# An fp32 transformer block on one core: the second MLP product in seven sub-products for eight, three more operands streamed from DRAM, and a new pool layout

## The chip, the core and the metric

The kernel runs on one core of a Trainium2 chip. The metric is the device time of one execution in microseconds (us), lower is better. Engines are named as in the profile: PE is TensorE (PEld its weight loads, which overlap its matmuls), DVE is VectorE, ACT is ScalarE, POOL is GpSimd, and SP issues the DMAs.

## The reference

Input is `x` of 1 x 2048 tokens x 576 features, fp32. `mod = silu(c) @ w_mod` gives six rows of 576. Then

```python
h = layernorm(x) * (1 + ca) + sa
x = x + ga * linear_attention(h, wqkv, wo)     # 32 heads of 18, q/k through a positive map
h = layernorm(x) * (1 + cb) + sb
x = x + gb * (silu(h @ w1) @ w2)               # w1: 576 x 4608, w2: 4608 x 576
```

The last line is the MLP, and the change is all in it: the "up product" is h @ w1, the "down product" silu(..) @ w2.

## The kernel before

Every product is made of three passes. An fp32 operand is split into a rounded part "hi" (an fp32r copy on ACT) and a remainder "lo" (a subtraction, `sub_hi`, L62, on DVE), and a product is hi.hi + hi.lo + lo.hi, accumulated in PSUM. So an operand costs one ACT copy and one DVE subtraction, and a 128 x 128 x n product costs three matmuls.

**Stages.** LayerNorm, q/k/v and attention take the first 370 us or so. In them the MLP's first 256 hidden features (group 0) are already worked off as filler. From about 403 us on only the MLP is left, for hidden groups g = 1 to 17 of 256 features each (`NG` is 18). The tokens are two pairs p = 0, 1 of 1024, and a pair is two blocks i = 0, 1 of 512. One (g, p) is a `Unit`; there are 34 of them. At the head of the file the result rows lie in SBUF as `acc` (16 tiles of 128 tokens x 576), and every unit's down product is added to them.

**Up product (L912).** It is already done by seven products instead of eight (a Strassen scheme in Winograd's form): the 2 x 2 parts are feature halves of h and token blocks on one side, feature halves and hidden halves of w1 on the other. `ORDER = (1, 6, 2, 5, 7, 3, 4)` is the order of the products. A product is 6 matmuls of 128 x 512, and four of the seven carry 2 more for the odd 64 features: 50 matmuls a unit. The token operands of pair 0 lie in DRAM (`hd`) and are fetched by SP into three rooms of 1 to 1.25 MB (`Unit.fetch`, L901), each when the room's last reader on PE is done; those of pair 1 stay in SBUF (`hr`). The w1 operands of a group are made by `sums` (four POOL subtractions of 128 x 256, L859 to L862) and `up` (an ACT copy and a DVE subtraction for each of seven). `act` (L954 to L957) adds the PSUM result to an earlier partial result on DVE, applies silu on ACT, and splits the 128 x 512 result `f` into `hs` for the down product (ACT copy, DVE subtraction).

**Down product (L966).** It is the plain one. For each of the unit's 8 token tiles: 2 halves of the 576 output columns x 2 hidden halves x 3 passes = 12 matmuls of 128 x 288, into a `down` PSUM tile of two banks (two such tiles), and then one DVE addition of 128 x 576 into `acc` (L969). w2 is scaled by `gb` on DVE (L878) and split by ACT and DVE in two pieces of 128 x 576 a group (L881).

**Order.** The down products of a unit run between the up products of the next one. The code asks for one up, one down, and so on, but the framework's planner lays out the queues by its own estimate of times: in the trace it is mostly two ups, then two downs. Each engine then works strictly in its queue's order. Only w1 of the next group is loaded and split while pair 1 runs; both w1 and w2 land in the one `raw` buffer of pool `wm`.

The kernel's functions:

Of the kernel before, what the change touches and what calls it, by code (L numbers as in the profile page):

```python
# [15 lines left out]
P = 128  # L16
# [5 lines left out]
def kernel(ctx: ExitStack, tc, A_x, A_wqkv, A_wo, B_x, B_w1, B_w2, c, w_mod, out):  # L22
# [658 lines left out]
    def store_h(n, view, at=0):  # L681
        nc.sync.dma_start(hd[n][:, at : at + view.shape[1], :], f32(view))
# [4 lines left out]

    def store_s(pair, S, p):
        if pair == 0:
            store_h(p, S)  # L690
        else:
            hr[p] = S
# [12 lines left out]
    def turn_all(tb):  # L705
# [16 lines left out]
        else:  # L722
# [3 lines left out]
            S = [wqp.tile([P, 4, 512], F32R, name="S", bufs=2) for _ in range(2)]  # L726
# [21 lines left out]
        if tb % 2 == 1:  # L748
            e, o = h2[tb - 1], h2[tb]
            if pair == 0:  # L750
                store_h(1, e[:, 0:4, :])
                store_h(2, e[:, 4:9, :])
                store_h(4, o[:, ODD : ODD + 5, :])
                store_h(5, o[:, 9:10, :], 4)
                store_h(3, e[:, DIFF : DIFF + 1, :], 4)
            for n, p in ((0, 5), (1, 6)):
                store_s(pair, S[n], p)
            pool = wqp if pair == 0 else h2p
            S = [pool.tile([P, 4, 512], F32R, name="S", bufs=2) for _ in range(2)]
            for n, p in ((0, 7), (1, 3)):  # L760
                for c in range(2):
                    split_s(S[n], c, h32s[:, 2 * n + c])
                store_s(pair, S[n], p)
                yield
# [60 lines left out]
    wts = [wm.tile([P, 2, FW], F32R, name=f"wt{i}") for i in range(2)]  # L825
    for wt in wts:
        G.memset(f32(wt[64:128, 1, :]), 0.0)

    hr[1], hr[2], hr[4] = h2[2][:, 0:4, :], h2[2][:, 4:9, :], h2[3][:, ODD : ODD + 5, :]
    hr_tail = {2: htail(2), 5: htail(3), 3: h2[2][:, DIFF, :], 4: htail(3)}  # L830
    rst = rs.tile([P, 3, 2, P], F32, name="t")
    rooms = [rs.tile([P, 5, 512], F32R, name=f"room{i}") for i in range(2)][::-1] + [h2[3][:, 0:5, :]]
    rooms_used = 0
# [9 lines left out]
    class Weights:  # L843


        def __init__(self, g):
            self.f0, self.wt, self.w1, self.w2 = g * FW, wts[g % 2], {}, []

        def load1(self):
            r1 = self.r1 = wm.tile([P, KC + 1, FW], F32, name="raw")  # L850
# [5 lines left out]
        def sums(self):  # L856
            b11, b12, b21, b22 = (self.r1[:, 2 * j : 2 * j + 2, k * P : (k + 1) * P] for j in range(2) for k in range(2))
            t = rst
            G.tensor_sub(t[:, 0], b22, b12)  # L859
            G.tensor_sub(b12, b12, b11)  # L860
            G.tensor_sub(t[:, 1], b22, b12)
            G.tensor_sub(t[:, 2], b21, t[:, 1])  # L862
            self.b = {1: b11, 2: b21, 3: b22, 4: t[:, 2], 5: b12, 6: t[:, 1], 7: t[:, 0]}
            tail_w(self.wt, self.r1[:, KC, :])

        def up(self, n):
            w = self.w1[n] = wm.tile([P, 4, P], F32R, name="w1", bufs=8)
            A.copy(w[:, 0:2], self.b[n])  # L868
            sub_hi(w[:, 2:4], self.b[n], w[:, 0:2])

        def load2(self):
            r2 = wm.tile([P, KC + 1, FW], F32, name="raw").rearrange("p k f -> p (k f)")[:, : G2 * D]
# [3 lines left out]
        def down(self):  # L876
            r2 = self.r2
            V.tensor_mul(r2, r2, bc["gb"].unsqueeze(1).to_broadcast([P, G2, D]))  # L878
            for j in range(G2):
                w = pg.tile([P, 2, D], F32R, name="w2", bufs=3)  # L880
                A.copy(w[:, 0], r2[:, j])  # L881
                sub_hi(w[:, 1], r2[:, j], w[:, 0])
                self.w2.append(w)

    class Unit:


        def __init__(self, pair, w, last):
            self.pair, self.w, self.last = pair, w, last
            self.h = {}  # L890

        def fetch(self, n):

            nonlocal rooms_used
            if self.pair == 1:
                self.h[n] = hr[n], hr_tail.get(n)
            else:
                room = rooms[rooms_used % len(rooms)]
                rooms_used += 1
                m = hd[n].shape[1]  # L900
                nc.sync.dma_start(f32(room[:, :m, :]), hd[n])  # L901
                self.h[n] = room, room[:, 4, :]

        def passes(self, n, ps, first, k=None):

            h, tail = self.h[n]
# [4 lines left out]
            for i, (left, right) in enumerate(seq):  # L911
                T.matmul(ps, left, right, start=first and i == 0, stop=i == len(seq) - 1, skip_group_check=True)  # L912

        def up(self, n):
            def temp(name):
# [134 lines left out]
```

## Time and profile before

| | |
|---|---|
| median of 3 runs | 1238.67 us (1236.83 to 1239.61) |
| the profiled execution | 1238.09 us, span 1236.4 us, granted clock 0.992 |
| instructions | 18508 |
| PE / DVE / ACT / POOL busy | 97% / 63% / 34% / 10% of the span |
| HBM read / written | 188.17 MB / 13.11 MB |

The span is the time from the first to the last record of the core; the execution takes 1.7 us more. Busy shares count time in which at least one instruction of the engine runs. "idle before" of a group of instructions is time in which its engine had nothing else to do, with the engine and line that ended it. A line number can be that of a helper: all splits' subtractions are L62. Instructions of one engine overlap a little in the records, so the cost of one more instruction is read from back-to-back rows.

### The profile page before, as it was taken

The numbers are of one execution on the slowest core, as the hardware profiler recorded it, in microseconds if no ns is written. First come the engines' busy times: TensorE is split into PE (matmuls) and PEld (weight loads), VectorE is DVE, ScalarE is ACT, GpSimd is POOL, SyncE is SP. The second block draws the span as 40 slices with busy tenths as digits, with TensorE's granted clock in tenths as the row PEclk, the third lists the DMA queues.
The fourth block names the chain that finished last, engine by engine and source line by source line (L and its number), as shares of the span: only waits on it lengthen the run. The fifth ranks groups of instructions, "written<-read, shape, count | busy, mean of one in ns | idle before, by whom it ended". The sixth has DMA issues, their size and how long they took to land.

```text
span 1236.4 us, 18508 instructions
## 1 busy us (share of the span) xinstructions
PE 1195.0 (97%) x7569; PEld 1105.7 (89%) x7569; DVE 773.9 (63%) x1284; ACT 417.4 (34%) x780; POOL 125.8 (10%) x132
## 2 busy tenths in 40 slices
PE   5999999999898899999999999999999999999998
PEld 4999999899896699999999999999999999999998
DVE  6756754888858456466575565665665755656655
ACT  5434342235545323233233232332332332323321
POOL 3200000421501001001011000000010100100000
PEclk9999999999988999999999999999999999999999
DMA  9212300213423855563653744745636537446423
GB/s 265 99 52 74 111 1 1 80 39 115 173 84 118 324 190 185 211 245 118 263 194 141 291 160 175 252 155 202 254 117 251 205 138 284 160 175 257 158 79 153
DMA packets 48115, 202.48 MB, mean 164 GB/s; under 512 B 4570, under 2 KB 16094, under 8 KB 31902
## 3 DMA queue, kind: packets, MB, share of 16 engines
q1 hardware_dynamic: 48030, 201.30, 45.1%
q8 instruction: 59, 0.97, 0.3%
q14 instruction: 26, 0.21, 0.1%
HBM read 188.17 MB, written 13.11 MB: 163 GB/s over the span
## 4 chain that ended last, share of the span: by engine, by line
PE 85%; DVE 5%; issue 5%; DMA 3%; ACT 2%; POOL 1%; SPq 0%; POOLq 0%; ACTq 0%; DVEq 0%
PE down L966 35%; PE up L912 31%; PE psK L154 9%; PE big L154 4%; PE small L641 1%; PE big L655 1%; PE kvp L390 1%; DVE hT L62 1%; DMA acc<-in_A_wqkv_dram 1%; DVE S L62 1%; DMA room<-hd 1%; DMA hT<-in_w_mod_dram 1%; DMA raw<-in_w_mod_dram 1%; PE psT L142 0%; PE big L566 0%
## 5 line engine op out<-in xcount | busy, mean ns | idle before, releaser
L966 PEld LDWEIGHTS down<-w,hs 128*128 128x128 f32 x3264 | 450.1, 188 | 16.6 <-ACT hs L957 2.8
L966 PE MATMUL down<-w,hs 128*128 128x288 f32 x3264 | 459.6, 295 | 2.3 <-ACT hs L957 2.3
L969 DVE TENSOR_TENSOR acc<-down,acc 128x576 f32<-128x576 f32 x272 | 204.9, 756 | 276.9 <-PE down L966 276.8
L912 PE MATMUL up<-hT,w 128*128 128x512 f32 x540 | 143.3, 392 | 0.0
L955 ACT ACTIVATE f<-f 128x512 f32<-128x512 f32 x102 | 64.5, 632 | 207.5 <-DVE f L954 207.5
L154 PE MATMUL psK<-w,hT 128*128 128x288 f32 (+2 forms) x896 | 125.3, 297 | 3.2 <-DVE e L129 1.2
L912 PE MATMUL up<-room,w 128*128 128x512 f32 x480 | 126.1, 393 | 1.5 <-DVE acc L657 0.9
L154 PEld LDWEIGHTS psK<-w,hT 128*128 128x128 f32 x896 | 120.8, 189 | 4.4 <-DVE hT L62 1.9
L912 PEld LDWEIGHTS up<-hT,w 128*128 128x128 f32 x540 | 99.9, 189 | 20.0
L912 PE MATMUL up<-S,w 128*128 128x512 f32 x408 | 110.6, 394 | 0.9 <-DVE f L954 0.9
L957 ACT CAST hs<-f 128x512 fp32r<-128x512 f32 x136 | 78.1, 619 | 92.8 <-PE down L966 92.7
L912 PEld LDWEIGHTS up<-room,w 128*128 128x128 f32 x480 | 86.3, 188 | 15.5 <-DVE acc L657 1.1
L62 DVE TENSOR_TENSOR hs<-f,hs 128x512 fp32r<-128x512 f32 x136 | 88.7, 683 | 0.1
L912 PEld LDWEIGHTS up<-S,w 128*128 128x128 f32 x408 | 74.7, 188 | 15.2 <-DVE f L954 1.3
L859 POOL TENSOR_TENSOR t<-raw 128x256 f32<-128x256 f32 x17 | 13.0, 767 | 713.7 <-DMA raw<-in_B_w_dram 488.7
L952 ACT ACTIVATE f<-up 128x512 f32<-128x512 f32 x34 | 20.3, 598 | 141.0 <-PE up L912 140.9
L154 PE MATMUL big<-w,qT 128*128 128x288 f32 x448 | 66.6, 303 | 0.8 <-DVE qT L62 0.7
L154 PEld LDWEIGHTS big<-w,qT 128*128 128x128 f32 x448 | 61.7, 192 | 1.6 <-DVE qT L62 1.0
L62 DVE TENSOR_TENSOR w<-raw,w 128x256 fp32r<-128x256 f32 (+2 forms) x104 | 58.9, 579 | 3.1 <-ACT w L868 2.1
L912 PE MATMUL up<-hT,wt 128*128 128x512 f32 x180 | 56.3, 393 | 0.0
L881 ACT CAST w<-raw 128x576 fp32r<-128x576 f32 x34 | 22.8, 674 | 76.3 <-PE down L966 51.8
L912 PEld LDWEIGHTS up<-hT,wt 128*128 128x128 f32 x180 | 33.9, 188 | 7.0
(188 smaller groups left out, 1276.9 us busy)
## 6 DMA issues: line engine op xcount, KB each, us to landing
room<-hd SPq DMA_DIRECT2D x46, 1280.0 KB, 5.5
room<-hd SPq DMA_DIRECT2D x34, 1024.0 KB, 5.9
hT<-hd SPq DMA_DIRECT2D x22, 1280.0 KB, 6.0
hT<-hd SPq DMA_DIRECT2D x17, 1024.0 KB, 4.7
raw<-in_B_w_dram SPq DMA_DIRECT2D x18, 576.0 KB, 3.6
raw<-in_B_w_dram SPq DMA_DIRECT2D x18, 512.0 KB, 3.6
xt<-in_A_x_dram SPq DMA_DIRECT2D x16, 288.0 KB, 4.3
raw<-in_w_mod_dram SPq DMA_DIRECT2D x8, 576.0 KB, 3.6
```

The source lines that it names most:

```text
L62: return V.tensor_sub(lo, full, f32(hi))
L154: T.matmul(ps, xpart(a), wpart(b), start=n == 0, stop=n == len(XW) - 1)
L390: T.matmul(o, vt[:, j, h, :], pkt[:, :, j * HG : j * HG + P], start=(t == 0 and h == 0 and j % 2 == 0), stop=(t == NT - 1 and h == 1), ski ...
L641: T.matmul(ps, left, right, start=n == 0, stop=n == len(seq) - 1)
L859: G.tensor_sub(t[:, 0], b22, b12)
L881: A.copy(w[:, 0], r2[:, j])
L912: T.matmul(ps, left, right, start=first and i == 0, stop=i == len(seq) - 1, skip_group_check=True)
L952: A.activation(f, ps, AF.Silu)
L955: A.activation(f, f, AF.Silu)
L957: A.copy(hs[:, 0], f)
L966: T.matmul(ps[:, h, :HALF], self.hs[i, k][:, a, tok], self.w.w2[k][:, b, h * HALF : (h + 1) * HALF], start=n == 0, stop=n == len(seq) - 1)
L969: V.tensor_add(halves(r), ps[:, :, :HALF], halves(r))
```

## The change

1. The down product too is done by seven products, in every unit and block but the very last one (g = 17, pair 1, block 1). The 2 x 2 parts are token halves of a block (256 each) and hidden halves (128) on one side, hidden halves and output column halves (288) of w2 on the other. A product is 6 matmuls of 128 x 288. A unit has 14 of them (`DOWN = (1, 7, 2, 4, 5, 6, 3)` for both blocks), two around each up product.
2. Each product is followed by one DVE addition of 128 x 576 out of PSUM, into a quarter of the result or into `U`, a new accumulator for what three quarters share. `U` is added to these three quarters once, at the end.
3. The operands are linear combinations. For a block POOL makes `s3`, two parts of `s` and `s4` (128 x 256 each), ACT makes the hi parts (`ha`, `hd`, `he` of 256 and `hb`, `hc` of 512), DVE subtracts for `ha` and `hb`, POOL for `hd`, `hc` and `he`. For w2 POOL does four subtractions of 128 x 288 a group, and ACT and DVE split seven pieces of 128 x 288 where there were two of 576.
4. Block 0's operands are made in the unit itself (after the third and the sixth up product), block 1's after the first up product of the next unit. The silu results `f` have one buffer each and are partly overwritten (`s4` in place).
5. Products 6, 2 and 5 of pair 1 also come from DRAM: ten fetches a group for seven. They are stored once, before the MLP stage. The next group's w1 is loaded at the start of pair 1 (before: during pair 0).
6. The pools of the MLP stage lie in another order. The first two operands have rooms of their own (`first`), released before the operand pool `ph` is laid over them; `h2p` is released earlier, and the room `rs` lies in its place.
7. In the last group results are stored by quarters (256 tokens x 288 columns) as they are ready, and the last block goes tile by tile as before.

```diff
-    hd = {n: dram.tile([P, 4 + (n in WITH_TAIL), 512], F32, name=f"hd{n}") for n in ORDER}
+    STREAM = [(0, n) for n in ORDER] + [(1, n) for n in (6, 2, 5)]
+    hd = {(q, n): dram.tile([P, 4 + (n in WITH_TAIL), 512], F32, name=f"hd{q}{n}") for q, n in STREAM}
...
-    for p in (px, rawp, pc, wp, wg):
+    for p in (px, rawp, pc, wp, wg, h2p):
         p.release()
...
+    w2p = tc.alloc_tile_pool(name="w2p", bufs=1, reuse_waits="tile")
+    wm = tc.alloc_tile_pool(name="wm", bufs=1, reuse_waits="tile")
     pf = tc.alloc_tile_pool(name="pf", bufs=1, reuse_waits="tile")
-    wm = tc.alloc_tile_pool(name="wm", bufs=1, reuse_waits="tile")
-    pg = tc.alloc_tile_pool(name="pg", bufs=1, reuse_waits="tile")
-    rs = tc.alloc_tile_pool(name="rs", bufs=1, reuse_waits="tile")
+    first = tc.alloc_tile_pool(name="first", bufs=1, reuse_waits="tile")
+    rs = tc.alloc_tile_pool(name="rs", bufs=1, side="right", reuse_waits="tile")
...
+    U = [pf.tile([P, 2, HALF], F32, name=f"U{b}") for b in range(NB)]
-    rooms = [rs.tile([P, 5, 512], F32R, name=f"room{i}") for i in range(2)][::-1] + [h2[3][:, 0:5, :]]
+    rooms0 = [first.tile([P, 4, 512], F32R, name=f"first{i}") for i in range(2)]
+    rooms = [h2[3][:, 0:5, :], h2[2][:, 4:9, :], rs.tile([P, 5, 512], F32R, name="room")]
...
+        def winograd(self, b11, b12, b21, b22, t):
+            G.tensor_sub(t[0], b22, b12)
+            G.tensor_sub(b12, b12, b11)
+            G.tensor_sub(t[1], b22, b12)
+            G.tensor_sub(t[2], b21, t[1])
+            return {1: b11, 2: b21, 3: b22, 4: t[2], 5: b12, 6: t[1], 7: t[0]}
...
-        def down(self):
+        def sums2(self):
             r2, t = self.r2, self.temps(HALF)
             V.tensor_mul(r2, r2, bc["gb"].unsqueeze(1).to_broadcast([P, G2, D]))
...
+            self.b2 = self.winograd(*parts, [t[:, i] for i in range(3)])
+        def split2(self, n, src):
+            w = self.w2[n] = w2p.tile([P, 2, HALF], F32R, name="w2", bufs=9)
+            A.copy(w[:, 0], src)
+            sub_hi(w[:, 1], src, w[:, 0])
+    def fetch(i):
+        if i < len(streamed):
+            _, q, n = streamed[i]
+            room = rooms0[i] if i < 2 else rooms[(i - 2) % 3]
...
+            if i is not None and i >= 2:
+                fetch(i + 3)
...
-            hs = self.hs[i, k] = pf.tile([P, 2, 512], F32R, name=f"hs{i}{k}")
-            A.copy(hs[:, 0], f)
-            sub_hi(hs[:, 1], f, hs[:, 0])
+        def split(self, i, name, src, *products, eng=V):
+            m = len(products)
+            t = ph.tile([P, m, 2, HT], F32R, name=f"{name}{i}")
+            A.copy(t[:, :, 0, :], src)
+            eng.tensor_sub(t[:, :, 1, :], src, f32(t[:, :, 0, :]))
...
+        def operands1(self, i):
+            half = self.half
+            self.split(i, "ha", half(i, 0, 0), 1)
+            s3 = pf.tile([P, 1, HT], F32, name="s3")
+            G.tensor_sub(s3, half(i, 0, 0), half(i, 0, 1))
+            self.split(i, "hd", s3, 7, eng=G)
+        def operands2(self, i):
+            half = self.half
+            s = pf.tile([P, 2, HT], F32, name="s")
+            G.tensor_add(s[:, 0:1], half(i, 0, 1), half(i, 1, 1))
+            self.split(i, "hb", half(i, 1, 0, 2), 2, 4)
+            G.tensor_sub(s[:, 1:2], s[:, 0:1], half(i, 0, 0))
+            self.split(i, "hc", s, 5, 6, eng=G)
+            s4 = half(i, 1, 0)
+            G.tensor_sub(s4, s4, s[:, 1:2])
+            self.split(i, "he", s4, 3, eng=G)
+        def down(self, m):
+            i, n = m // 7, self.DOWN[m % 7]
+            b = 2 * self.pair + i
+            if n in (1, 5):
+                banks = [down_bank(), down_bank()]
+                self.x, self.y = banks[::-1] if i else banks
+            ps = self.x if n in (1, 2, 5, 3) else self.y
+            for p in range(2):
+                for j, (u, v) in enumerate(((0, 0), (0, 1), (1, 0))):
+                    T.matmul(ps[:, p, :HALF], self.a[i, n][:, u, p * P : (p + 1) * P], self.w.w2[n][:, v],
+                             start=n in (1, 5, 7, 6) and j == 0, stop=j == 2, skip_group_check=True)
+            dst = {1: U[b], 6: U[b], 7: self.c(b, 1, 1), 5: self.c(b, 1, 1), 2: self.c(b, 0, 0),
+                   4: self.c(b, 1, 0), 3: self.c(b, 0, 1)}[n]
+            V.tensor_add(dst, ps[:, :, :HALF], dst)
+            if self.last:
...
         for q, n in enumerate(ORDER):
+            if before:
+                before.down(2 * q)
             unit.up(n)
             if before:
-                before.down(q)
+                before.down(2 * q + 1)
+                if q == 0:
+                    before.operands1(1)
+                    before.operands2(1)
+            if p == 0 and q == 1:
+                unit.w.sums2()
+            if q == 2:
...
+                unit.operands1(0)
+            if q == 5:
+                unit.operands2(0)
+            if p == 0:
+                unit.w.down(*{2: (1, 7), 4: (2, 4), 5: (5, 6), 6: (3,)}.get(q, ()))
+            if p == 1 and more:
+                ws[g + 1].up(n)
+        if p == 1 and more:
+            ws[g + 1].load2()
+        before = unit
+    unit.plain_operands(1)
+    unit.add_u(3, (1, 1), (1, 0), (0, 1))
+    for m in range(7):
+        unit.down(m)
+    for t in range(4):
+        unit.plain_down(1, t)
```

More of the change, by code (lines that the diff above doesn't have):

```diff
@@ L885 @@
-    class Unit:
[L888 to L896, printed above, removed]
-            else:
[L898 to L906, printed above, removed]
+            parts = [r2[:, j, k * HALF : (k + 1) * HALF] for j in range(2) for k in range(2)]
@@ L948, in act @@
[L948 to L971 removed]
+                self.passes(4, self.bank_b, False, 0)
@@ L978 @@
     w.load2()
[L979 to L999 removed]
+    for i in range(5):
+        fetch(i)
@@ L1000 @@
+    for u in U:
+        G.memset(u, 0.0)
+    ws = {1: w}
+    ph, before = None, None
+    units = [(g, p) for g in range(1, NG) for p in range(2)]
+    for g, p in units:
+        unit = Unit(g, p, ws[g])
+        more = g + 1 < NG
+        if p == 1 and more:
+            ws[g + 1] = Weights(g + 1)
+            ws[g + 1].load1()
+            ws[g + 1].sums1()
         for q, n in enumerate(ORDER):
-            if n not in unit.h:
-                unit.fetch(n)
+            if before:
+                before.down(2 * q)
```

254 lines of the change are left out of this document (129 added, 125 removed).

## The prediction

> **What bounds the kernel now.** I read the page's busy shares, then the chain that ended last, then stretches of the MLP stage by engine.
>
> ```profile
> PE 1195.0 (97%) x7569; PEld 1105.7 (89%) x7569; DVE 773.9 (63%) x1284; ACT 417.4 (34%) x780; POOL 125.8 (10%) x132
> ```
>
> The chain, in order of time (start, length, what):
>
> ```profile
> 807.15 3.46 PE up L912 x15
> ...
> 855.57 3.46 PE up L912 x15
> ...
> 1210.34 22.31 PE down L966 x168
> ```
>
> Two stretches, one about pair 1 and one about pair 0 of a group (PE, PEld, DVE, ACT, POOL busy, clock, DMA share, GB/s):
>
> ```profile
> 800.50:824.70 24.20, 24.20 (x144) 21.83 (x143) 14.98 (x25) 8.08 (x18) 3.07 (x4) 1.00 0.24 84
> 824.70:848.90 24.20, 24.20 (x152) 22.35 (x151) 14.32 (x22) 6.32 (x12) 0.00 (x0) 1.00 0.86 318
> ```
>
> PE has no gap here and the chain between 800 and 910 us is PE alone. A group repeats after 855.57 - 807.15 = 48.42 us. A down matmul costs 22.31 / 168 = 0.1328 us (not the row's 295 ns, which overlap), so 192 of them cost 25.50, and the 100 up matmuls the other 22.92: 0.229 each. DVE is busy 14.98 + 14.32 = 29.3 us of 48.4, POOL 3.07. The 16 DMA engines are at 0.86 while pair 0 streams, at 0.24 otherwise.
>
> Groups of instructions, by shape:
>
> ```profile
> L969 DVE TENSOR_TENSOR acc<-down,acc 128x576 f32<-128x576 f32 x272 | 204.9, 756 | 276.9 <-PE down L966 276.8
> L62 DVE TENSOR_TENSOR hs<-f,hs 128x512 fp32r<-128x512 f32 x136 | 88.7, 683 | 0.1
> L957 ACT CAST hs<-f 128x512 fp32r<-128x512 f32 x136 | 78.1, 619 | 92.8 <-PE down L966 92.7
> L868 ACT CAST w<-raw 128x256 fp32r<-128x256 f32 x68 | 25.9, 403 | 24.4 <-DMA raw<-in_B_w_dram 23.2 <-PE up L912 0.9
> L736 POOL TENSOR_TENSOR H<-H,sl 128x512 f32<-128x512 f32 x2 | 2.6, 1296 | 0.2
> ```
>
> DVE and POOL side by side (start, length):
>
> ```profile
> 868.22 0.97 DVE L62 TENSOR_TENSOR w<-raw,w 128x256 fp32r<-128x256 f32 x1
> 869.12 0.95 DVE L62 TENSOR_TENSOR wt<-raw,wt 64x256 fp32r<-64x256 f32 x1
> 870.00 0.68 DVE L954 TENSOR_TENSOR f<-up,u 128x512 f32<-128x512 f32 x1
> 870.60 0.41 DVE L62 TENSOR_TENSOR w<-t,w 128x256 fp32r<-128x256 f32 x1
> 870.93 0.75 DVE L62 TENSOR_TENSOR w<-raw,w 128x256 fp32r<-128x256 f32 x2
> ```
> ```profile
> 868.17 0.74 POOL L860 TENSOR_TENSOR raw<-raw 128x256 f32<-128x256 f32 x1
> 868.99 0.80 POOL L861 TENSOR_TENSOR t<-raw 128x256 f32<-128x256 f32 x1
> 869.87 0.80 POOL L862 TENSOR_TENSOR t<-raw,t 128x256 f32<-128x256 f32 x1
> ```
>
> While POOL works, a DVE subtraction of 256 out of SBUF takes 0.95 to 0.97 instead of 0.41; an addition that reads PSUM keeps its 0.68.
>
> **The change, part by part.**
>
> *Down matmuls.* 33 units go from 96 to 84, the last to 42 + 48 = 90: 33 x 12 + 6 = 402 fewer, all on the path: 402 x 0.1328 = -53.4 us. Shape and number of weight loads per matmul stay. A group would take 48.42 - 24 x 0.1328 = 45.23 us. The rest of the sum is whether others keep that pace.
>
> *DVE.* A second instruction in a back-to-back row costs 0.67 (576 elements: two in 1.42), 0.60 (512: 1.28) and 0.33 (256: 0.75); 288 I take at 0.36. Per group: 28 additions for 16, +8.0; operands of the four blocks 0.33 + 0.60 each instead of eight of 0.60, -1.1; w2 seven times 0.36 for two of 0.67, +1.2. From 29.3 to 37.4 of 45.2 us, 83%. With POOL beside it, the subtractions and the multiplication that read SBUF only (3.7 operands, 3.8 w2, 3.1 w1: 10.6 us) are stretched: POOL will work about 73% of the time, the stretch seen is up to 2.3 times, I take 1.6: +4.6, 42 us, 93%. Hidden by PE, but not freely: product k uses the bank of k - 2 and waits for its addition. Between lie one up product (6 x 0.229 = 1.37) and one down product (0.80), 2.17 us, of which the addition takes 0.76; so 1.4 us of other work may stand in front of it in DVE's queue. The w2 multiplication (1.36, more beside POOL) and two operand subtractions can exceed that. No trace shows this. Bounds: 0 (before, PE never waits) and 1.6 us a group (one multiplication stretched to twice overshoots by 1.3, one more wait 0.3). I take 0.5, nearer to the row without waits, since DVE's load is still under PE's: +9 us over 17 groups, 0 to +27.
>
> *ACT.* Copies: per block three of 256 at 0.40 and two of 512 at 0.62 for two of 0.62, per group +4.8; w2 +1.6. From 14.4 to some 21 of 45 us, hidden. If a copy of a POOL result is late, the silu behind it is late; `f` has several us of slack, so 0.
>
> *POOL.* Per group 24 operand and 4 w1 operations of 256, four of 512, four of 288. Spacing 0.82 to 0.88 for 256, 1.38 for 512, 0.93 for 288: 28 x 0.85 + 5.5 + 3.7 = 33 us of 45, 73%. They form chains: for a block `s3`, its hi copy on ACT, `hd`; `s`, copy, `hc`; `s4`, copy, `he`; the whole takes some 7 us (6 x 0.85 + 1.4, and a copy that nothing covers). The code leaves time for it: block 0's last input is there after the sixth up product, and `he` is used 13 us later (one up product of 1.8, two more of 1.4, six to eight down products of 0.8, and the next); block 1 has 12 us until its product 7. So 0 on the path; what it costs if this cover goes is a rival below. The sum goes by the rows, 0.74 to 0.80 for 256. The Trainium skill's GPSIMD Engine Reference, section 4.1 (Engine selection), advises VectorE for elementwise work with two inputs, as about twice as fast; by its 4497 ns for 2048 elements (section 3.1) an estimate, taken per element, is 0.56 for 256 and some 22 us a group.
>
> *SP and DMA.* Three more fetches, 1024 + 1280 + 1280 KB, raise a group from about 9.7 to 13.4 MB, in 45.2 us 295 GB/s; 318 GB/s went with share 0.86, so 0.80 on average. A room's next fetch is issued as its product ends and needed two ups and six downs or so later: 3.5 + 4.8 = 8 us; a 1280 KB fetch landed in 5.5 to 6.0. Pair 1's three have 11 us, and SP's load of w1 waits in front of no fetch that is due sooner. 0 on the path.
>
> *Start of the stage.* Before, the first unit waits for fetches: the chain has 6.85 us of DMA into a room whose memory the filler's last down product still used. Rooms `first` may be free earlier (-6 at best); against it, pair 1 has three resident products fewer to fill such a wait with (+4). Neither shows; I take 0. The clearing of `U` is four short writes while POOL idles 25 us, and the three operands' stores (3584 KB) lie in stretches with 109 GB/s: 0.
>
> *End.* After the last up product come 1 + 7 products and 4 tiles, 96 matmuls, 12.7 us, with no up product between: each addition has 0.80 us of PE against 0.67 to 0.76, and six additions of `U` and two splits come on top on DVE (5.2 us, part of it earlier). Bounds 0 and +4, I take +2. The last store stays as long.
>
> Sum, against the profiled execution's 1238.1 (0.6 below the median): -53.4 + 9 + 0 + 2 = **1195.7, say 1196**; own range 1238.1 - 53.4 - 6 = 1179 to 1238.1 - 53.4 + 27 + 4 + 4 = 1220.
>
> **Rivals.**
>
> *POOL takes DVE's time (faster, but little).* If every SBUF-only DVE instruction of the stage is doubled, DVE has 37.4 + 10.6 = 48.0 us a group and becomes the bound: 1238.1 - 53.4 + 17 x (48.0 - 45.23) + 2 = 1234. At 1.9 times it has 46.9, which gives 1216. So some 1220 to 1236. For it: the rows at 868 us. Against it: POOL is idle a quarter of the time. The Trainium skill's GPSIMD Engine Reference, section 1 (Specifications), says that Pool's SBUF interfaces are shared with VectorE and contended for by its instructions with two SBUF inputs; the trace agrees (0.95 against 0.41, PSUM readers untouched).
>
> *POOL's queue becomes the bound (slower).* Its subtractions also stretch beside DVE: at 389 to 392 us, beside 512-wide ones, 256 took 1.06 to 1.18. With 1.2 spacing, 28 x 1.2 + 4 x 1.9 + 4 x 1.35 = 46.6, and if POOL idles 0.6 us for each of its 12 hi copies a group, 53.8. It decides from 48.4 on. Then DVE's writes into `f`, which wait for `he`, hold up the down additions behind them. At 51 us a group: 1238.1 - 53.4 + 17 x (51 - 45.23) + 2 = 1285. Against it: the mean over all w1 rows is 0.80, and other POOL work can fill the waits.
>
> *Fetches late.* Pair 0's stretch already has share 0.86 and would have to move as much and the w2 load in 22.6 us. If its four tight fetches are half a us late each, 2 us a group, 34 in all: about 1230. Against it: after 24 us come 20 with few fetches, and no PE wait for DMA is seen in any steady group.
>
> *It does less, or more, than it says:* the number of matmuls follows from the code; only the start of the stage could give a few us more than 6.
>
> **Chances.** Forecast 0.61; POOL taking DVE's time 0.15; POOL's queue 0.17; fetches 0.05; below 1179 0.02. The range 1178 to 1232 holds the first, the fetches and most of the second, 0.80. 0.2% (2.5 us) is about what a measurement of this kernel can tell from no change. Faster: 0.61 + 0.13 + 0.05 + 0.02 = 0.81; same 0.02 (the upper end of the second); slower 0.17.
>
> **What would show it.** A group's period near 45.5 with PE still the whole chain confirms the main step; gaps before down matmuls released by DVE's addition give the size of the third; DVE over 95% in a group, with 256 and 288 subtractions at 0.7 or more, is the first rival; POOL without idle time, or PE waiting for `he` or `hc`, the second; PE waiting for a room, the fetches. I am wrong above all if the planner's queue order, made from its own times, lets DVE or ACT stand behind a POOL result that comes later than planned.

## The result: slower, and where the time came from

The changed kernel takes 1279.06 us (median of 4 runs, 1275.75 to 1283.97); the kernel before took 1239.01 in the same runs. The ratio is 1.033 [1.0294, 1.0366]: slower by 3.3%, where 1196 was forecast. The profiled execution takes 1279.52 us with a span of 1277.7.

The page of the kernel after, its busy line and the first line of the chain that ended last, then that line of the chain of the kernel before:

```profile
PE 1190.5 (93%) x7167; PEld 1061.4 (83%) x7167; DVE 958.4 (75%) x1583; ACT 522.3 (41%) x1067; POOL 599.8 (47%) x673
PE 53%; DVE 19%; DMA 10%; issue 7%; POOL 7%; ACT 3%; SPq 0%; POOLq 0%; ACTq 0%; DVEq 0%
```
```profile
PE 85%; DVE 5%; issue 5%; DMA 3%; ACT 2%; POOL 1%; SPq 0%; POOLq 0%; ACTq 0%; DVEq 0%
```

The 402 matmuls are gone (7569 before, 7167 now), but PE's busy time fell only from 1195.0 to 1190.5, and in the chain PE's share went from 85% to 53% and DVE's from 5% to 19%. No other engine is full: DVE is busy 75%.

The stretch from 520 to 1000 us of the kernel after, then of the kernel before (length; PE, PEld, DVE, ACT, POOL busy, with counts; granted clock, DMA share, GB/s):

```profile
520.00:1000.00 480.00, 454.82 (x2543) 391.98 (x2542) 373.69 (x593) 198.88 (x432) 296.38 (x341) 1.00 0.69 264
```
```profile
520.00:1000.00 480.00, 480.00 (x2900) 438.27 (x2899) 289.64 (x448) 144.61 (x279) 31.60 (x40) 1.00 0.55 201
```

Before, PE was busy 480.00 of these 480 us. The granted clock is 1.00 in both, so it isn't the cause. A group's period, read as the mean spacing of ACT's `p<-up` copies (one a unit, every second one counted) over groups 4 to 16, is 50.46 us; before it is 48.44, and 45.23 was forecast.

Splitting both spans at the first and the last of these copies places the whole loss. To the first: 407.0 against 404.5 us, +2.5. Between them: 813.67 against 786.75, +26.9. From the last to the end of the span: 57.03 against 45.15, +11.9. Together +41.3, which is the difference of the spans, 1277.7 - 1236.4.

Who makes PE wait? The waits of PE and its weight loads in the kernel after, over the whole span (total us, times, longest):

```profile
PEld down L1029 <- DVE acc L1033: 38.1, 91, 1.9
...
PE down L1029 <- DVE acc L1033: 18.4, 34, 2.5
...
PEld down L1029 <- DVE U L1033: 12.3, 19, 2.8
...
PE up L941 <- DMA hT<-hd: 10.2, 11, 1.7
...
PE down L1029 <- DVE U L1033: 9.5, 16, 2.6
```

Four of the five are down products waiting for the DVE addition (L1033) that empties a PSUM bank. Before, the only such wait between 520 and 1000 us was this one:

```profile
PEld down L966 <- DVE acc L969: 0.3, 1, 0.3
```

The timeline of the kernel after shows the place. PE (start, length, what):

```profile
779.61 0.61 PE L941 MATMUL up<-room,wt 128*128 128x512 f32 x2
780.07 1.74 PE L1029 MATMUL down<-w,hc 128*128 128x288 f32 x12
781.87 1.06 PE L1029 MATMUL down<-w,he 128*128 128x288 f32 x6
782.90 1.06 PE L1029 MATMUL down<-w,ha 128*128 128x288 f32 x6
783.80 1.05 PE L1029 MATMUL down<-w,hd 128*128 128x288 f32 x6
784.90 1.04 PE L1029 MATMUL down<-w,hb 128*128 128x288 f32 x6
785.77 1.61 PE L941 MATMUL up<-S,w 128*128 128x512 f32 x6
```

DVE at the same place:

```profile
781.05 0.76 DVE L1033 TENSOR_TENSOR acc<-down,acc 128x576 f32<-128x576 f32 x1 [0.90 <-PE down L1029]
781.73 0.45 DVE L62 TENSOR_TENSOR w<-raw,w 128x288 fp32r<-128x288 f32 x1
782.09 0.75 DVE L1033 TENSOR_TENSOR U<-down,U 128x576 f32<-128x576 f32 x1
782.97 0.76 DVE L1033 TENSOR_TENSOR acc<-down,acc 128x576 f32<-128x576 f32 x1
783.99 0.76 DVE L1033 TENSOR_TENSOR U<-down,U 128x576 f32<-128x576 f32 x1 [0.27 <-PE down L1029]
```

Six down products stand in one row, with no up product between. The code has at most two in a row. The 36 matmuls take 785.77 - 780.07 = 5.70 us, against 36 x 0.1328 = 4.78. In such a row each bank is wanted again when one other product has run, 12 x 0.1328 = 1.59 us after the product that filled it began. But that product's records end 0.95 us after its start, and the addition takes 0.76 more. The third product here starts at 781.87, 1.80 us after the first and 0.06 after the first one's addition has ended, although DVE had stood idle for 0.90 us before that addition. So in a row PE is late even where DVE is free; a 0.45 us split between the additions makes it later. Without a wait the records of a product last 0.94 to 0.96 us and the next one starts 0.79 to 0.80 after the start. Here they last up to 1.06, the next starts 0.90 to 1.10 later, and there is next to no gap: PE's busy time contains part of the stall, and so it hardly fell.

Counted over PE's whole queue, 453 of the 469 down products stand ahead of the last up product, and 216 of those in 31 rows of six to eight. The planner made them. In these rows the second product starts 0.81 us behind the first in the mean, and every later one at least 0.89 and 1.06 in the mean behind the one before it. By the starts of PE's records and the 0.1328 us of a down matmul, the rows lose about 43 us between the first and the last copy. Its queue also leaves 16 products behind the last up product, where the code has 8.

The end shows the same wait at its largest. DVE, then PE, of the kernel after:

```profile
1248.68 3.07 DVE L1047 TENSOR_TENSOR acc<-acc,U 128x576 f32<-128x576 f32 x3
```
```profile
1252.47 3.23 PE L1029 MATMUL down<-w,hb 128*128 128x288 f32 x12 [2.60 <-DVE U L1033]
```

In the row of 16, three additions of `U`, which PE doesn't wait for, stand in front of an addition that PE waits for: 2.60 us of PE.

### The profile page after: what moved, and what is told of

Same layout as the page of the kernel before. It is cut to its first block, busy times and chain, and to the rows that moved or that the text cites. A ratio compares the mean times of both kernels' runs of the same rounds, so it can differ in the third digit from the quotient of the medians.

```text
span 1277.7 us, 19286 instructions
## 1 busy us (share of the span) xinstructions
PE 1190.5 (93%) x7167; PEld 1061.4 (83%) x7167; DVE 958.4 (75%) x1583; ACT 522.3 (41%) x1067; POOL 599.8 (47%) x673
## 4 chain that ended last, share of the span: by engine, by line
PE 53%; DVE 19%; DMA 10%; issue 7%; POOL 7%; ACT 3%; SPq 0%; POOLq 0%; ACTq 0%; DVEq 0%
PE up L941 21%; PE down L1029 15%; PE psK L154 8%; DVE acc L1033 5%; DMA hT<-hd 5%; DVE w L62 4%; PE big L154 4%; DMA raw<-in_B_w_dram 2%; DVE hb L990 2%; PE big L655 1%; PE small L641 1%; DVE f L979 1%; POOL t L862 1%; POOL hc L990 1%; PE kvp L390 1%
## 5 line engine op out<-in xcount | busy, mean ns | idle before, releaser
L1033 DVE TENSOR_TENSOR acc<-down,acc 128x576 f32<-128x576 f32 x335 | 250.6, 751 | 86.7 <-PE down L1029 83.3
L941 PE MATMUL up<-hT,w 128*128 128x512 f32 x876 | 231.0, 397 | 14.0 <-DMA hT<-hd 10.2
L1029 PE MATMUL down<-w,hc 128*128 128x288 f32 x804 | 128.2, 300 | 8.2 <-DVE acc L1033 6.9
L1029 PE MATMUL down<-w,hb 128*128 128x288 f32 x804 | 128.8, 300 | 7.2 <-DVE U L1033 4.6
L1029 PEld LDWEIGHTS down<-w,hc 128*128 128x128 f32 x804 | 115.9, 189 | 21.9 <-DVE acc L1033 13.8
L1029 PEld LDWEIGHTS down<-w,hb 128*128 128x128 f32 x804 | 117.5, 191 | 16.9 <-ACT ha L989 3.9
L1033 DVE TENSOR_TENSOR U<-down,U 128x576 f32<-128x576 f32 x134 | 100.8, 752 | 18.1 <-PE down L1029 16.3
L990 POOL TENSOR_TENSOR hc<-s,hc 128x512 fp32r<-128x512 f32 x67 | 87.3, 1303 | 31.8 <-ACT hc L989 31.3
L62 DVE TENSOR_TENSOR w<-raw,w 128x288 fp32r<-128x288 f32 (+2 forms) x139 | 76.3, 557 | 10.2 <-ACT w L883 7.6
L1029 PE MATMUL down<-w,he 128*128 128x288 f32 x402 | 68.4, 305 | 8.4 <-DVE acc L1033 7.8
L1029 PE MATMUL down<-w,ha 128*128 128x288 f32 x402 | 66.1, 300 | 5.3 <-DVE U L1033 4.8
```

The costliest lines, as they stand in the source:

```text
L62: return V.tensor_sub(lo, full, f32(hi))
L941: T.matmul(ps, left, right, start=first and m == 0, stop=m == len(seq) - 1, skip_group_check=True)
L990: eng.tensor_sub(t[:, :, 1, :], src, f32(t[:, :, 0, :]))
L1029: T.matmul(ps[:, p, :HALF], self.a[i, n][:, u, p * P : (p + 1) * P], self.w.w2[n][:, v], start=n in (1, 5, 7, 6) and j == 0, stop=j == 2, ...
L1033: V.tensor_add(dst, ps[:, :, :HALF], dst)
```

## The experiments

The theory, T1: the loss is the planner's rows of down products, in which each product waits for DVE's addition to free its bank. The rivals, numbered as in the expectations: T2, DVE has too much to do with 28 additions a group; T3, POOL's work, by stretching DVE's instructions or by chains that come late; T4, the three more fetches. The kernels with thin additions, without the fetches or without POOL's operand work leave out a part of the work or use other operands, so they only serve to find the cause. All ratios are to the kernel before, run beside each kernel. "Pinned" means that PE's queue follows the code's order; the other queues stay the planner's.

| kernel | us | ratio | period, us |
|---|---|---|---|
| after | 1279.06 | 1.033 [1.0294, 1.0366] | 50.46 |
| PE pinned | 1217.83 | 0.9847 [0.9822, 0.9871] | 46.71 |
| without the three fetches | 1273.69 | 1.0292 [1.0266, 1.0317] | 50.38 |
| thin additions | 1222.31 | 0.9876 [0.9857, 0.9896] | 47.03 |
| without POOL's operand work | 1262.05 | 1.0198 [1.0157, 1.0238] | 49.40 |
| PE pinned, without POOL's operand work | 1192.55 | 0.9632 [0.9601, 0.9664] | 45.36 |
| PE pinned, thin additions | 1208.1 | 0.9758 [0.9725, 0.9791] | 46.45 |
| PE pinned, without the three fetches | 1240.09 | 1.0016 [0.9998, 1.0034] | 48.17 |
| PE pinned, splits held back | 1237.02 | 1.0002 [0.9981, 1.0023] | 48.04 |
| PE pinned, rows of seven written out | 1460.46 | 1.18 [1.1736, 1.1864] | 62.75 |
| PE and DVE pinned | 1381.0 | 1.1153 [1.1126, 1.118] | 56.47 |
| PE, DVE and ACT pinned | 1530.41 | 1.2351 [1.2315, 1.2388] | 65.89 |
| the kernel before, PE pinned | 1241.38 | 1.0037 [1.002, 1.0054] | 48.41 |
| PE pinned, `ha` on POOL | 1214.4 | 0.9812 [0.9782, 0.9842] | 46.59 |
| PE pinned, `ha` and `hb` on POOL | 1223.35 | 0.9889 [0.9866, 0.9911] | 47.12 |
| PE pinned, `ha` on POOL, multiplication in two | 1231.65 | 0.9963 [0.9945, 0.998] | 47.78 |

### PE in the code's order

```diff
     units = [(g, p) for g in range(1, NG) for p in range(2)]
-    for g, p in units:
+    with tc.manual_schedule(engines={mybir.EngineType.PE}):   # loop and end of the stage
+        for g, p in units:
```

> PE alone issues the MLP stage in the order in which the code emits it: two down products, one up product. The other queues stay the planner's. Theory 1 (order): in the changed kernel PE's queue holds up to eight down products in a row, and in such a row each has to wait for the DVE addition of the one two before it, in the same PSUM bank. With the rows gone a group should take 45.5 to 47 us and the whole 1195 to 1220 us. Theory 2 (DVE is too loaded with 28 additions a group) and theory 3 (POOL's operands come too late, or slow DVE down): the order is not the cause, so PE only waits elsewhere, and the time stays at 1260 or above. Theory 4 (fetches): the same, above 1255.

Measured: 1217.83 us, 61 less than the kernel after, and 1.5% faster than the kernel before. The work is the same, in another order. The same stretch of the kernel with PE pinned:

```profile
520.00:1000.00 480.00, 470.05 (x2745) 417.90 (x2744) 416.81 (x636) 213.31 (x461) 321.41 (x370) 1.00 0.79 286
```

It does 2745 matmuls in this stretch, where the kernel after does 2543, although its DVE is busier (417 us for 374), its POOL too, and the DMA share is 0.79 for 0.69. None of these three was the limit, and T2 falls: all of DVE's additions are still there. Its waits over the whole span:

```profile
PEld down L1029 <- DVE U L1033: 14.8, 16, 1.6
...
PE down L1029 <- DVE U L1033: 11.3, 29, 1.2
...
PE down L1029 <- DVE acc L1033: 6.9, 6, 1.9
```

T1 holds for 61 us; the 43 us of the rows above and the 15 by which the end gets shorter nearly make them up. The end from the last copy takes 41.8 us instead of 57.0. What is left is 1217.8 - 1192.6 = 25 us above the kernel without POOL's work below.

### Without the three fetches

```diff
-    STREAM = [(0, n) for n in ORDER] + [(1, n) for n in (6, 2, 5)]
+    STREAM = [(0, n) for n in ORDER]
...
+    hr[6], hr[2], hr[5] = hr[7], hr[3], hr[4]
```

> Pair 1's products 6, 2 and 5 read other resident token operands and are not fetched, so their results are those of other operands: seven fetches a group as before. Theory 4 (three more fetches a group make the up products late): 1200 to 1225 us. Theory 1 (PE's order): the planner's order for this kernel still has rows of seven and eight down products, one for each unit, so 1260 to 1280. Theories 2 and 3: 1265 to 1280, since DVE and POOL have the same work.

Measured: 1273.69 us. The period is 50.38 for 50.46, so the three fetches are not the cause; T4 falls. The fetches do land later in the kernel after than before. Issue to landing (us, at the end of the line), for the kernel after, this one, and the kernel with PE pinned, which makes all ten fetches:

```profile
hT<-hd SPq DMA_DIRECT2D x69, 1280.0 KB, 7.5
```
```profile
hT<-hd SPq DMA_DIRECT2D x46, 1280.0 KB, 7.1
```
```profile
hT<-hd SPq DMA_DIRECT2D x69, 1280.0 KB, 5.5
```

A fetch of 1280 KB lands in 7.5 us, where 5.5 to 6.0 was read before; the room was about 8, and PE waited for these fetches 10.2 us in the whole span. It isn't the amount of traffic: between 520 and 1000 us the core moves 264 GB/s in the kernel after, 193 in this one, and 286 with PE pinned, where a fetch lands in 5.5. The late landing comes with the planner's PE order; how was not looked into.

### Thin additions

```diff
-            V.tensor_add(dst, ps[:, :, :HALF], dst)
+            V.tensor_add(dst[:, :, :32], ps[:, :, :32], dst[:, :, :32])
```

> Each down product's addition takes only 32 of 288 columns of each half, the rest of the result is left out; about 0.13 to 0.2 us instead of 0.75. DVE loses some 15 us of work a group. Theory 2 (DVE's load): 1190 to 1215 us. Theory 1 (order, with the wait for the addition two products before): also much faster, 1195 to 1225, since a short addition ends the wait in any order; this run tells 1 and 2 from 3 and 4, which expect above 1255.

Measured: 1222.31 us, in the planner's own order. With the addition short, the rows cost little: a second way to remove the same wait, with nearly the same gain (57 us for 61). It takes work from DVE as well, so it can't tell T1 from T2 by itself; pinning, which leaves DVE its work, does. Both ends of "rows of products, each of which waits for an addition" are needed.

### Without POOL's operand work, in both orders

```diff
             A.copy(t[:, :, 0, :], src)
-            eng.tensor_sub(t[:, :, 1, :], src, f32(t[:, :, 0, :]))
+            if eng:
+                eng.tensor_sub(t[:, :, 1, :], src, f32(t[:, :, 0, :]))
...
-            s3 = pf.tile([P, 1, HT], F32, name="s3")
-            G.tensor_sub(s3, half(i, 0, 0), half(i, 0, 1))
-            self.split(i, "hd", s3, 7, eng=G)
+            self.split(i, "hd", half(i, 0, 1), 7, eng=None)
...
-            self.split(i, "hc", s, 5, 6, eng=G)
+            self.split(i, "hc", half(i, 0, 0, 2), 5, 6, eng=None)
...
-            self.split(i, "he", s4, 3, eng=G)
+            self.split(i, "he", half(i, 1, 0), 3, eng=None)
```

> POOL does nothing for the down operands: products 7, 5, 6 and 3 take plain quarters of the silu result without the sums and differences, and their rounded part stands in for the remainder; matmuls, ACT copies and DVE work are the same in number. Theory 3 (POOL's chains or its contention with DVE): 1195 to 1225 us. Theory 1: the planner's order still has rows of six and seven down products, so 1250 to 1275, a little better because DVE's SBUF-only subtractions are no longer stretched (some 4 us a group of DVE time). Theory 2: 1260 to 1280.

> PE in the code's order and POOL without work for the down operands (products 7, 5, 6 and 3 take plain quarters, and their rounded part stands in for the remainder). With PE's order pinned a group still took 46.6 us instead of 45.23. If that rest is DVE's SBUF-only subtractions stretched by POOL (0.99 and 1.0 us for 256 elements ahead of an addition that PE waits for), the group falls to 45.2 to 45.5 and the whole to 1188 to 1202 us. If it is DVE's plain number of instructions, 1210 to 1218.

Measured: 1262.05 us in the planner's order, 1192.55 with PE pinned. With the kernels that keep POOL's work this makes a square: pinning is worth 61 us with POOL's work and 70 without it; POOL's work costs 17 us in the planner's order and 25 with PE pinned. So T3 is real and the smaller part, and it alone would not have made the kernel slower than before.

With PE pinned and no POOL work PE is full. Its stretch:

```profile
520.00:1000.00 480.00, 479.51 (x2838) 433.12 (x2837) 404.40 (x658) 216.60 (x477) 74.47 (x86) 1.00 0.80 292
```

The period is 45.25 us in most groups (45.36 in the mean), and the forecast had 45.23: the matmuls removed are worth what was said, once nothing makes PE wait.

What POOL does to DVE is seen in groups of instructions by shape, between 520 and 1000 us. With PE pinned and POOL's work in place (count, busy us and mean ns, idle before):

```profile
L990 DVE TENSOR_TENSOR ha<-f,ha 128x256 fp32r<-128x256 f32 x41 | 34.6, 845 | 3.1 <-ACT ha L989 2.7
...
L62 DVE TENSOR_TENSOR w<-t,w 128x256 fp32r<-128x256 f32 x32 | 19.6, 612 | 0.0
```

and without it:

```profile
L62 DVE TENSOR_TENSOR w<-t,w 128x256 fp32r<-128x256 f32 x33 | 13.6, 411 | 0.0
...
L991 DVE TENSOR_TENSOR ha<-f,ha 128x256 fp32r<-128x256 f32 x43 | 24.6, 572 | 0.0
```

The same subtraction takes 612 ns in the mean beside POOL and 411 without; half of them keep some 0.41 us, and the longest takes 1.00. `ha` takes 845 and 572 (one of the 41 took 3.46 us), but the w2 split from `raw` 489 and 512, so not every row is stretched. The Trainium skill's GPSIMD Engine Reference, section 1 (Specifications), says that the two engines contend for shared SBUF interfaces when VectorE's instruction has two inputs in SBUF. The subtractions have two, and the rows shown agree. How it reaches PE is seen at 572 us, with PE pinned. POOL, DVE and PE (start, length, what):

```profile
572.67 0.74 POOL L865 TENSOR_TENSOR t<-raw,t 128x256 f32<-128x256 f32 x1
573.37 0.92 POOL L990 TENSOR_TENSOR hd<-s,hd 128x256 fp32r<-128x256 f32 x1
```
```profile
572.70 0.99 DVE L62 TENSOR_TENSOR w<-t,w 128x256 fp32r<-128x256 f32 x1
573.62 1.29 DVE L62 TENSOR_TENSOR w<-raw,w 128x256 fp32r<-128x256 f32 x2
...
575.43 0.41 DVE L62 TENSOR_TENSOR w<-t,w 128x256 fp32r<-128x256 f32 x1
575.76 0.75 DVE L1033 TENSOR_TENSOR U<-down,U 128x576 f32<-128x576 f32 x1
```
```profile
576.56 1.85 PE L1029 MATMUL down<-w,hb 128*128 128x288 f32 x12 [0.53 <-DVE U L1033]
```

While POOL works, DVE's subtraction takes 0.99 us; once it is still, 0.41. The addition behind them comes late, and PE stands for 0.53.

### Pinned, with thin additions

This is the pinning and the thin addition in one kernel.

> PE in the code's order, and each down addition takes 32 of 288 columns of each half only (the rest of the result is left out). All waits of PE for DVE should be gone whatever their cause: 45.2 us a group, 1188 to 1200 us in all. If it stays above 1210, the rest is not DVE's but lies at the start of the stage or in fetches. Beside the same short additions in the planner's order (1222) it also tells what that order costs when additions are short: nothing by a theory in which only the bank wait counts, so both alike; 20 us or more if rows of down products cost something else too (up products that come late).

Measured: 1208.1 us, above the expected band. Between 520 and 1000 us PE waits here most for:

```profile
PEld down L1029 <- ACT he L989: 10.2, 9, 1.6
...
PE down L1029 <- DVE U L1033: 8.9, 10, 1.4
```

`he` is the last of POOL's chains in a block, and PE waits for it about once a group. So short additions don't buy back all that POOL costs: where they are short, its results come late, as the second rival had it. In the pinned kernel with whole additions no wait of PE for `he` is listed between 520 and 1000 us. There DVE waits for it before it writes the next `f`, 18.5 us in this stretch, and PE has no wait right behind that:

```profile
L965 DVE TENSOR_TENSOR f<-up,p 128x512 f32<-128x512 f32 x21 | 14.4, 684 | 6.1 <-POOL he L990 5.3 <-PE up L941 0.8
L958 DVE TENSOR_TENSOR f<-up,p 128x512 f32<-128x512 f32 x21 | 14.3, 682 | 13.2 <-POOL he L990 13.2
```

So how the 25 us divide between stretching and lateness was not settled. Against the thin additions in the planner's order (1222.3), pinning is still worth 14 us.

### Rows of seven, written out

The opposite of pinning the code's order: PE pinned to rows of seven down products, behind the second and the sixth up product.

```diff
         for q, n in enumerate(ORDER):
-            if before:
-                before.down(2 * q)
             unit.up(n)
             if before:
-                before.down(2 * q + 1)
+                if q in (1, 5):
+                    for m in range(7):
+                        before.down(7 * (q // 5) + m)
```

> PE's order is given by the code too, but with all seven down products of a block in a row, twice a unit, between the up products: what the planner did for half of the products is done for all. Theory 1 (in a row each down product waits for the addition of the one two before it): a row of seven takes 1.5 to 3 us more than its 5.6 us, four rows a group, so 51 to 57 us a group and 1280 to 1390 us in all. If the rows were harmless and pinning helped for another reason (up products earlier, fetches), 1215 to 1235.

Measured: 1460.46 us, beyond the expected band. The waits over the whole span:

```profile
PE down L1029 <- DVE acc L1033: 75.8, 100, 3.4
...
PE down L1029 <- DVE U L1033: 44.8, 48, 3.1
...
PE up L941 <- DMA hT<-hd: 29.9, 13, 2.7
```

The direction is T1's: PE now waits for additions 121 us (75.8 + 44.8), where it was 28 (18.4 + 9.5) in the kernel after. By the starts of PE's records a row of seven takes 3.2 us more than its matmuls, just above the 1.5 to 3 expected. But the up products now also stand in rows and outrun the fetches (29.9 us), and the granted clock was 0.94 between 520 and 1000 us, where it is 1.00 in the kernel after. So the size is not that of the rows alone.

### The kernel before, with PE pinned

The same line around the loop of the kernel before.

> The kernel before, with PE alone in the order in which its code emits the MLP stage (one up, one down tile of 12 matmuls). Theory 1: there a down tile takes 1.59 us, longer than an addition, so rows of two or four tiles cost nothing and there is nothing to gain: 1236 to 1242 us. If the planner's PE order is worth 20 us or more by itself, 1220 or less.

Measured: 1241.38 us, 1.0037 [1.002, 1.0054] of the kernel before. The planner's order wasn't harmful there. Ahead of the last up product it has at most two down tiles in a row, so this run doesn't test long rows; but the 14 tiles behind it follow each other without a wait, 168 matmuls in 22.31 us (the third line of the chain in the prediction). With 12 matmuls, 1.59 us, to one addition of 0.76, a bank is empty before it is wanted. The change halved the product per addition, and the planner made longer rows of these products; the two together became expensive.

### DVE, and ACT, in the code's order too

```diff
+    with tc.manual_schedule(engines={mybir.EngineType.PE, mybir.EngineType.DVE}):
```

> PE and DVE both issue in the code's order. In the code's order a down addition comes directly behind its product's place, and the splits of w1 and w2 behind the additions. If planned DVE order (three splits of w1 in a row ahead of an addition) is what is left of the loss, 1190 to 1208 us; if DVE then stands behind results of POOL and ACT that come later than the code's place for them, 1225 or more.

> PE, DVE and ACT in the code's order. ACT then makes hi parts of POOL's results before later silus: if POOL's results are late for that, ACT holds up the silus and DVE, and the time is above the run with PE and DVE pinned, by 5 us or more; if not, the two are within 3 us of each other.

Measured: 1381.0 and 1530.41 us. Pinning further engines undid everything. The waits of the first over the whole span:

```profile
PE down L1029 <- DVE U L1033: 120.8, 49, 8.0
...
DVE wt L62 <- ACT wt L618: 94.0, 16, 7.4
```

In the code's order DVE stands up to 7.4 us behind a split whose ACT copy comes late, and the additions stand behind it, up to 8.0 us for PE. The order in which the code makes operands is no order for the engine that makes them. The granted clock was lower in these two as well, 0.955 and 0.902 over the span for 0.989 in the kernel after, so not all of their loss need be waiting; the two parts were not separated.

### Pinned, without the three fetches; pinned, with the splits held back

The first is the pinning and the edit without the three fetches. The second also ties the splits of w1 and w2 to stand behind the step's last down addition in DVE's queue:

```diff
+                    last_add = before.down(2 * q + 1)
...
+                with behind([last_add] if before else []):
+                    unit.w.down(*{2: (1, 7), 4: (2, 4), 5: (5, 6), 6: (3,)}.get(q, ()))
```

> PE in the code's order, and pair 1's products 6, 2 and 5 read other resident operands (their results are then those of other operands), so seven fetches a group. If the three additional fetches cost nothing on the path, as forecast, the time is that of the run with PE's order alone pinned, 1218, within 4 us. If late fetches are what is left there, 1195 to 1208.

> PE in the code's order, and on DVE the splits of the next w1 and of w2 are queued behind the last down addition of the step in which the code emits them, so that they no longer stand three or four in a row ahead of an addition. If bursts of splits are the rest of the loss, 1200 to 1212 us; if it is DVE's and POOL's total, 1214 to 1222.

Measured: 1240.09 and 1237.02 us, both some 20 us worse than pinning alone, and both misses. The kernel with fewer fetches can't be slower for its fetches; its DVE timeline shows what changed:

```profile
732.12 1.65 DVE L894 TENSOR_TENSOR raw<-raw,bc_gb 128x1152 f32<-128x1152 f32 x1 [0.72 <-DVE w L62]
...
735.62 1.54 DVE L62 TENSOR_TENSOR w<-raw,w 128x288 fp32r<-128x288 f32 x1
```

The `gb` multiplication and a stretched w2 split came to stand right in front of additions, and PE lost 0.79 and 0.80 us behind them. Every edit makes the planner lay DVE's queue anew, and here the place of these few long instructions moved the period by about 1.5 us. So what the fetches cost with PE pinned can't be read from this run.

### `ha` on POOL; `ha` and `hb`; the multiplication in two

```diff
-            self.split(i, "ha", half(i, 0, 0), 1)
+            self.split(i, "ha", half(i, 0, 0), 1, eng=G)
```

and in the second also `hb` with `eng=G`; in the third, with `ha` alone, the multiplication by `gb` as two instructions of half the length.

> PE in the code's order, and POOL instead of DVE subtracts for operand ha (four times 256 elements a group). DVE loses four instructions that took 0.85 us each beside POOL, POOL gains four of 0.8. If DVE's load is the rest of the loss, 1205 to 1214 us; if POOL's queue is, 1220 to 1235.

> PE in the code's order, and POOL subtracts for ha and hb too: DVE has no operand subtraction of the block left (3.7 us a group of 37 less before any stretch), POOL has 33 + 4 x 0.85 + 4 x 1.4 = 42 us a group of about 46. If DVE is the limit, 1200 to 1212; if POOL's queue then is, 1218 to 1250.

> PE in the code's order, POOL subtracts for ha, and the multiplication of w2 by gb is two DVE instructions of 576 elements for one of 1152, so that an addition can go between. If the longest DVE instruction makes the waits, 1204 to 1211; if not, 1212 to 1218 as without it.

Measured: 1214.4, 1223.35 and 1231.65 us. The first is the fastest kernel here that computes the whole result, but its interval overlaps that of pinning alone (0.9812 [0.9782, 0.9842] and 0.9847 [0.9822, 0.9871]). With `hb` there as well POOL is busy 394 of the 480 us between 520 and 1000, and the kernel is slower than with `ha` alone. The Trainium skill's GPSIMD Engine Reference, section 4.1 (Engine selection), would give elementwise work with two inputs to VectorE. Here the run with one operand moved away from it can't be told from pinning alone, and the run with the second one is 9 us slower than that. The third was meant to let an addition go between the two halves and came out 17 us worse than `ha` alone. Its DVE timeline shows that the planner left them together, again in front of an addition that PE waits for:

```profile
536.20 2.19 DVE L894 TENSOR_TENSOR raw<-raw,bc_gb 128x576 f32<-128x576 f32 x2
538.31 0.74 DVE L1034 TENSOR_TENSOR U<-down,U 128x576 f32<-128x576 f32 x1
```

So it doesn't test what it was meant to. A hand-made order of DVE was not tried.

## Why the prediction was wrong, point by point

*The matmuls, -53.4 us: right.* The pinned kernel without POOL's operand work has a period of 45.25 us in most groups for the forecast 45.23.

*DVE, +9 us (0 to +27): the step that failed.* It had the mechanism, "product k uses the bank of k - 2 and waits for its addition", and then took from the code that one up product and one down product lie between, 2.17 us, with 1.4 to spare. PE's queue isn't the code's. In a row of six to eight, only one down product lies between: the bank is wanted 1.59 us after the product that filled it began, and at 780 us the addition had emptied it, and the next product could start, only after 1.80. So nothing is to spare. The text before the prediction said itself that the planner had put two ups and then two downs; the step used the code's order all the same, and didn't ask what the planner would do with products half as long. Measured against the pinned kernel without POOL's operand work, the kernel after takes 87 us more of span: 1.9 before the first copy, 67.6 up to the last, 17.8 from there on. Pinning PE alone takes 61 us off the run. Also, "DVE's load is still under PE's" was true and no reason for so small a value: DVE was 75% busy and on the chain nonetheless, because what counts is when an addition runs, not how much DVE has to do.

*DVE stretched beside POOL (1.6 times): the right mechanism, mis-sized.* 612 ns for 411 and 845 for 572 in the mean are 1.5 times, but `hb`'s 835 for 685 is 1.2, and 489 for 512 no stretch. It costs 17 to 25 us together with POOL's late chains, where the term's 9 us was to cover all of DVE's waits.

*ACT, 0: nothing against it.* It is busy 199 of 480 us in the kernel after.

*POOL, 33 us of 45: right in size.* POOL works 321 of 480 us with PE pinned, 67%. That its chains cost 0 is not quite right: PE waits for `he` once a group where the additions are short.

*Fetches, 0: right, by less than it looked in the planner's order.* There landing took 7.5 us of the 8 there were, and leaving the three out moved the period by 0.08 us. With PE pinned it took 5.5, as forecast, and PE waited 2.8 us for these fetches in the whole span.

*Start, 0 (-6 to +4):* it came 2.5 us later, within the bounds.

*End, +2 (0 to +4): mis-sized.* The span from the last unit's first copy grew by 11.9 us over before, and it is 17.8 above the kernel that lacks the rows and POOL's work. Sixteen products stood there in a row for the code's eight, with the additions of `U` between DVE's. The term set an addition of 0.67 to 0.76 against the 0.80 us of one product, where a row needs 0.89 or more a product. With PE pinned the same end takes 41.8 us for 57.0.

*The rivals.* The slower one, at 1285 us, gave nearly the measured time, but by luck: its reason is another. POOL is idle 184 of 480 us, and without its work the kernel is still slower than before. DVE as the bound by stretching (1234) names the 17 to 25 us that are left when PE is pinned. The last sentence of what would make the prediction wrong looked at the planner's queues, but for DVE and ACT behind POOL; it was PE's own queue.

## What to carry to other kernels

Read the distance between two uses of a PSUM bank from the queue that the planner writes, not from the code, and compare it with the time of the instruction that empties the bank; when a change halves the work per bank, this slack is the first thing to go. A bound engine can lose time to one that is only 75% busy, and its own busy time then hides part of the wait. If the code's order keeps the distance, pin the bound engine alone: here that turned 3.3% slower into 1.5% faster, while pinning the engines that feed it as well made it 11.5 to 23.5% slower.

## What the runs showed that was not expected

- A down product that costs 0.80 us shows in the records as 0.95 us without a wait and as 1.04 to 1.06 in the planner's rows, with next to no idle time between, so PE was "93% busy" while a group took 5.2 us more than PE's work.
- Edits that have nothing to do with DVE's order (fewer fetches, a multiplication in two halves) moved the pinned kernels by some 17 to 22 us, through the place of two or three long instructions in DVE's queue. A single edit's gain under this planner is uncertain by that much unless the queue is looked at.
- The change's own gain, with the wait removed, is larger than what the best version keeps: without POOL's operand work, where PE is full, it takes 1192.55 us, and the best kernel run that computes the whole result takes 22 us more.
